# An attention, ELU and expert kernel: attention pairs in undivided blocks, y loads on another queue

## Chip, cores and metric

The kernel runs on one core of a Trainium2 chip. The metric is the device time of one execution in microseconds; a profiled execution gives the trace that is read here.

## What is computed

Three stages follow each other. Attention with a kernel feature map gives 2304 rows of 512; these go through an ELU layer of 2048 hidden units, and the result through four experts of 1024 hidden units, whose outputs are summed with weights.

```python
def phi(x):
    proj = np.einsum('bhsd,df->bhsf', x, w_phi)
    proj = proj - np.max(np.abs(proj), axis=-1, keepdims=True)
    return np.concatenate([np.exp(proj), np.exp(-proj)], axis=-1)
q_p, k_p = phi(q), phi(k)
kv = np.einsum('bhsf,bhsd->bhfd', k_p, v)
z = np.sum(k_p, axis=2)
num = np.einsum('bhsf,bhfd->bhsd', q_p, kv)
den = np.einsum('bhsf,bhf->bhs', q_p, z)[..., None] + 1e-06
attn = num / den                        # 4 batches, 8 heads, 576 rows, 64 columns
...
h = x @ w_in
g = np.where(h > 0.0, h, np.exp(np.minimum(h, 0.0)) - 1.0)
x = g @ w_out
...
p = domain_probs / (domain_probs.sum(-1, keepdims=True) + 1e-09)
for e in range(4):
    out += p[:, e:e + 1] * (np.maximum(x @ w1[e], 0.0) @ w2[e])
```

## The kernel before

Attention works on 16 pairs of heads. For a pair, `mid` projects the last 64 rows of queries and keys together (L229), `keys` and `queries` project the other 512 rows of each into two banks (L237), and for each of these a guard on VectorE subtracts the largest absolute value of a row (L211, L212). ScalarE takes the exponentials of the keys (`kexp`, L215 and L216). `kv` multiplies them with the values (L266, L267), and ScalarE copies the sums to `kvw` (L270). `tpose` transposes the guarded queries (L277, L281), and ScalarE takes their exponentials into `ew` on the way out (L286). `den` multiplies `ew` with the column sums (L295) and `num` with the value part (L308); ScalarE copies both out (`dd` L297, `nd` L309). `den` then sends `dd` to the tile `dn` by a small transfer (L299). `rec` takes the reciprocal on VectorE (L314, L315) and stores it, `spread` loads it back over all partitions into `rb` (L321), and `put_x` multiplies (L327), rounds to `xh` and `xl` (L333, L336) and stores the result. The next pair's queries and keys are loaded inside `queries` into a tile with a single buffer.

The generator `attention` writes these steps out for three pairs at a time: `new` is the youngest, `a` the one ahead of it, `z` the one ahead of that. It yields `True` three times a pair. Pairs 0 to 3 run in a prologue, where TensorE has nothing else, until four results are put; with the fourth, the first ELU tile can run. After that, attention is driven from the ELU units: each unit, 24 matmuls of layer one (L545 to L547) and 24 of layer two (L575 to L577), calls `slot` four times. A slot adds the rate to a quota and runs the generator to its next `True` for each whole one (`RHEAD` for the first two tiles of 256 rows, `RATE` up to tile 5), up to a limit of pairs per tile. A tile has four units; tiles 0 and 1 are interleaved. Slots also drive the conversion of the 64-bit ELU weights, which goes over ScalarE (L121, L122, L155), VectorE (L125 to L130) and GpSimd (L132, L134, L157).

The code is written in that order, and a scheduler then sets each engine's queue from priorities and its own times, so steps can move past each other. TensorE's results go through seven banks, and an ELU tile holds two of them as accumulators.

In the last stage a step is one expert and one group of 768 rows: seven products (L673 to L675) in the place of eight for the first matrix, then `Down` for the second (L777 to L779). For every expert but the first, `Down.run` loads the old sum `y` with a transfer that ScalarE's queue issues (L773), at the moment when the first product of these rows is written; `drain` adds (L787) and stores (L788). The y tiles have four buffers. Expert weights come in over SyncE's queue (`wst`, L480 and L508) and are split on ScalarE and GpSimd (L501, L502, L514, L515).

Of the kernel before, what the change touches and what calls it, by code (L numbers as in the profile page):

```python
# [43 lines left out]
PRE = 0.7  # L44
RATE = 0.375
RHEAD = 0.525
WRATE = 3
# [22 lines left out]
def attn_elu_moe_kernel(ctx: ExitStack, tc: tile.TileContext, kq_in, vv, w_phi, w_in, w_out, probs, w1, w2, out):  # L70
# [150 lines left out]
    class Pair:  # L221
# [4 lines left out]
        def mid(self):  # L226
            self.md = a1.tile([P, 2, P], F32, tag="md", name="md")
            pm = bank()
            pmark[0] = PE.matmul(pm[:, :2 * FEAT], self.kq[:, 512:640], wbd, start=True, stop=True).ins  # L229
            guard(self.md, pm, 2)  # L230
# [110 lines left out]
    def attention():  # L341
        a = new = None
        for i in range(B * NP + 2):
            z, a, new = a, new, Pair(i) if i < B * NP else None
            if a:
                a.kv(0)
                yield False
            if z:
                z.rec()
            if a:  # L350
                a.tpose(0)
                a.kv(1)
                yield False
                a.tpose(1)
                a.tpose(2)
            if new:
                new.mid()
            if a or new:
                yield True
            if z:  # L360
                z.spread()
                yield True
            if new:
                keys = new.keys()
                next(keys)
                yield False
                next(keys, None)
                yield False
            if z:
                z.put_x()  # L370
                done[0] += 1
                yield not new
            if new:
                qs = new.queries()
                next(qs)
                yield False
                next(qs, None)
                yield True
            if a:
                a.den()  # L380
                yield False
                a.num()
                yield False

# [377 lines left out]
    class Down:  # L762
        def __init__(self, e, g, s, j):
            self.e, self.s, self.j = e, s, j
            self.r = (2 * g + s) * NTT + j
            self.acc = None

        def run(self, q):
            if self.acc is None:
                self.acc = bank()  # L770
                self.y = yp.tile([P, DM], F32, tag="y", name="y", bufs=YB)
                if self.e:
                    A.dma_start(self.y, yscr[self.r])  # L773
            c = slice(self.j * P, (self.j + 1) * P)
# [14 lines left out]

    hs = {}  # L790
    xcur = [None]
    steps = [(e, g) for e in range(E) for g in (range(NG) if e % 2 == 0 else range(NG - 1, -1, -1))]
# [140 lines left out]
    for k, (e, g) in enumerate(steps):  # L933
# [8 lines left out]
        for q in range(NQ):  # L942
            if k == q == 0:
                continue
            ups[q].middle()
            slot()
# [89 lines left out]
```

## Time and profile before

| | before |
|---|---|
| median of 3 runs | 1375.21 us (1374.79 to 1375.89) |
| profiled execution | 1369.1 us |
| its span, first to last instruction | 1367.3 us |
| TensorE busy | 1343.6 us |
| VectorE busy | 653.8 us |
| ScalarE busy | 593.9 us |
| GpSimd busy | 353.7 us |

The busy times are of the span; 1.8 us of the profiled execution lie around it. A busy TensorE says that a matmul was in flight, and not that it ran at full speed. Weight loads overlap with matmuls and stand in the profile as an engine of their own, PEld. One matmul of 32-bit data in the attention stage stands as two records.

### The profile page before, as it was taken

How to read it: one execution, taken by the hardware profiler on the slowest of the kernel's cores; microseconds unless marked ns; L12 is line 12 of the kernel's file. 1: busy time of each engine (PE TensorE's matmuls, PEld its weight loads, DVE VectorE, ACT ScalarE, POOL GpSimd, SP SyncE). 2: the span in 40 equal slices, each digit the busy share in tenths (PEclk: the TensorE clock that was granted, in tenths of full speed). 3: DMA queues.
4: the chain of work that ended last, by engine and by line, in shares of the span. 5: the costliest groups of instructions: out<-in, count | busy, mean ns of one | idle time of the engine just before them, and what ended most of it. 6: DMA issues, size and time to landing. Idle time of an engine off the chain costs nothing.

```text
span 1367.3 us, 21606 instructions
## 1 busy us (share of the span) xinstructions
PE 1343.6 (98%) x8408; PEld 1222.4 (89%) x8408; DVE 653.8 (48%) x1085; ACT 593.9 (43%) x1268; POOL 353.7 (26%) x353
## 2 busy tenths in 40 slices
PE   8899999999999999999999999999999999999998
PEld 6788898988999999989888888989898988889897
DVE  5697546564755756683342433233432333433223
ACT  6687555565467554744333351213331213422121
POOL 2487422222454111364110360001420003500000
PEclk9999999999999999999999999999999999999999
DMA  7723344434424313275332155261354241543511
GB/s 245 219 84 94 109 124 155 131 106 125 133 83 123 110 30 121 103 243 177 139 115 106 31 164 194 82 209 44 124 170 162 100 154 31 163 155 99 198 57 62
DMA packets 98422, 173.43 MB, mean 127 GB/s; under 512 B 32272, under 2 KB 45712, under 8 KB 98320
## 3 DMA queue, kind: packets, MB, share of 16 engines
q1 hardware_dynamic: 83392, 148.25, 33.0%
q10 hardware_dynamic: 14928, 23.80, 5.4%
q8 instruction: 66, 1.08, 0.3%
q14 instruction: 36, 0.29, 0.1%
HBM read 118.13 MB, written 53.81 MB: 126 GB/s over the span
## 4 chain that ended last, share of the span: by engine, by line
PE 62%; issue 23%; DVE 3%; DMA 2%; POOL 2%; ACT 1%; SPq 0%; ACTq 0%; POOLq 0%; DVEq 0%
PE bank L673 7%; PE bank L675 7%; PE bank L674 7%; PE bank L777 5%; PE bank L778 5%; PE bank L779 5%; PE bank L266 3%; PE bank L756 2%; PE bank L754 2%; PE bank L755 2%; PE bank L576 2%; PE bank L577 2%; PE bank L545 2%; PE bank L575 2%; POOL w L502 2%
## 5 line engine op out<-in xcount | busy, mean ns | idle before, releaser
L673 PE MATMUL bank<-xv,w 128*128 128x384 f32 x840 | 280.8, 336 | 2.4 <-ACT cm L679 1.2
L674 PE MATMUL bank<-xv,w 128*128 128x384 f32 x840 | 281.6, 335 | 0.0
L675 PE MATMUL bank<-xv,w 128*128 128x384 f32 x840 | 281.5, 336 | 0.0
L778 PE MATMUL bank<-w,h 128*128 128x512 f32 x576 | 227.0, 394 | 0.0
L777 PE MATMUL bank<-w,h 128*128 128x512 f32 x576 | 226.1, 398 | 0.3 <-ACT h L689 0.2
L779 PE MATMUL bank<-w,h 128*128 128x512 f32 x576 | 200.5, 395 | 0.0
L502 POOL TENSOR_TENSOR w<-wst,w 128x256 fp32r<-128x256 f32 x100 | 80.4, 818 | 415.1 <-ACT w L501 415.0
L673 PEld LDWEIGHTS bank<-xv,w 128*128 128x128 f32 x840 | 157.7, 188 | 10.9 <-ACT cm L679 1.9
L674 PEld LDWEIGHTS bank<-xv,w 128*128 128x128 f32 x840 | 157.7, 188 | 6.4 <-POOL xv L624 0.2
L675 PEld LDWEIGHTS bank<-xv,w 128*128 128x128 f32 x840 | 157.6, 188 | 0.1
L689 ACT ACTIVATE h<-bank 128x384 fp32r<-128x384 f32 x144 | 67.8, 489 | 162.4 <-PE bank L675 103.3
L690 DVE SCALAR_TENSOR_TENSOR h<-bank,h 128x384 fp32r<-128x384 f32 x144 | 78.1, 555 | 116.2 <-ACT h L689 115.9
L777 PEld LDWEIGHTS bank<-w,h 128*128 128x128 f32 x576 | 107.8, 188 | 23.3 <-ACT h L689 1.3
L778 PEld LDWEIGHTS bank<-w,h 128*128 128x128 f32 x576 | 108.3, 188 | 22.2
L779 PEld LDWEIGHTS bank<-w,h 128*128 128x128 f32 x576 | 107.6, 188 | 22.2
L687 DVE TENSOR_TENSOR c<-cmab,bank 128x384 f32<-128x384 f32 x48 | 26.6, 554 | 197.5 <-ACT cmab L679 197.5
L679 ACT ACTIVATE cmab<-bank 128x384 f32<-128x384 f32 x60 | 29.4, 490 | 185.4 <-PE bank L675 185.4
L545 PE MATMUL bank<-xh,w 128*128 128x256 f32 x288 | 83.4, 289 | 4.0 <-DVE kp L212 2.2
L624 POOL TENSOR_TENSOR xv<-xs,xv 128x768 fp32r<-128x768 f32 x24 | 46.6, 1943 | 149.7 <-ACT xv L623 143.5
L575 PE MATMUL bank<-gh,w 128*128 128x256 f32 x288 | 82.0, 285 | 0.0
L546 PE MATMUL bank<-xl,w 128*128 128x256 f32 x288 | 81.2, 282 | 0.2 <-POOL xl L336 0.2
L576 PE MATMUL bank<-gl,w 128*128 128x256 f32 x288 | 80.6, 280 | 0.7 <-DVE gl L558 0.7
(118 smaller groups left out, 2531.5 us busy)
## 6 DMA issues: line engine op xcount, KB each, us to landing
xv<-xvd SPq DMA_DIRECT2D x42, 768.0 KB, 4.2
wst<-in_w SPq DMA_DIRECT2D x64, 256.0 KB, 2.8
xvd<-xv SPq DMA_DIRECT2D x21, 768.0 KB, 5.0
yscr<-y SPq DMA_DIRECT2D x54, 256.0 KB, 2.4
y<-yscr ACTq DMA_DIRECT2D x54, 256.0 KB, 2.9
kq<-in_kq SPq DMA_DIRECT2D x16, 320.0 KB, 3.2
rb<-rec SPq DMA_DIRECT2D x32, 144.0 KB, 3.0
xscr<-nd ACTq DMA_DIRECT2D x16, 288.0 KB, 2.8
```

The source lines that it names most:

```text
L502: on[WL[v % len(WL)]].tensor_tensor(out=lo, in0=x, in1=f32(hi), op=ALU.subtract)
L545: PE.matmul(ph[:, j], w[:, 0, c], xh[:, kc], start=(kc == j == 0), stop=False)
L546: PE.matmul(ph[:, j], w[:, 0, c], xl[:, kc], start=False, stop=False)
L575: PE.matmul(o, w[:, 0, c], self.gh[:, j], start=start, stop=False)
L576: PE.matmul(o, w[:, 0, c], self.gl[:, j], start=False, stop=False)
L673: PE.matmul(o, hi[:, c], x[:, 0, kc], start=not more and kc == 0, stop=False, skip_group_check=more)
L674: PE.matmul(o, hi[:, c], x[:, 1, kc], start=False, stop=False, skip_group_check=more)
L675: PE.matmul(o, lo[:, c], x[:, 0, kc], start=False, stop=kc == 1, skip_group_check=more)
L690: mark[0] = V.scalar_tensor_tensor(out=h[:, 1], in0=c, scalar=0.0, in1=f32(h[:, 0]), op0=ALU.max, op1=ALU.subtract).ins
L777: PE.matmul(self.acc, h[:, 0, c], w[:, 0], start=f == 0, stop=False)
L778: PE.matmul(self.acc, h[:, 0, c], w[:, 1], start=False, stop=False)
L779: PE.matmul(self.acc, h[:, 1, c], w[:, 0], start=False, stop=f == 2 * NQ - 1)
```

## The change

One iteration of `attention` is put in another order. It ran value products of `a`, its transposes, `mid` and `keys` of `new`, `queries` of `new`, and then denominators and numerators of `a`, with `rec`, `spread` and `put_x` of `z` and three yields between. Now it runs value products of `a`, `mid` and `keys` of `new`, denominators and numerators of `z`, transposes of `a`, `queries` of `new`, and only then, with the three yields, `rec`, `spread` and `put_x` of `z`. Denominators and numerators are thus computed one iteration later, and all matmuls of an iteration lie between two yields of `True`. `md` gets a second buffer, and both rates are higher. In the last stage `Down.load` takes over the y load: it goes to SyncE's queue, at the start of a step for the first half of the rows and two quarters later for the second, and three tiles of the x pool serve as y buffers beside the four.

```diff
-RATE = 0.375
-RHEAD = 0.525
+RATE = 0.55
+RHEAD = 0.7
...
-            self.md = a1.tile([P, 2, P], F32, tag="md", name="md")
+            self.md = a1.tile([P, 2, P], F32, tag="md", name="md", bufs=2)
...
             if a:
                 a.kv(0)
                 yield False
-            if z:
-                z.rec()
-            if a:
-                a.tpose(0)
                 a.kv(1)
                 yield False
-                a.tpose(1)
-                a.tpose(2)
             if new:
                 new.mid()
-            if a or new:
-                yield True
-            if z:
-                z.spread()
-                yield True
-            if new:
                 keys = new.keys()
                 next(keys)
                 yield False
                 next(keys, None)
                 yield False
             if z:
-                z.put_x()
-                done[0] += 1
-                yield not new
+                z.den()
+                yield False
+                z.num()
+                yield False
+            if a:
+                a.tpose(0)
+                a.tpose(1)
+                a.tpose(2)
             if new:
                 qs = new.queries()
                 next(qs)
                 yield False
                 next(qs, None)
+            yield True
+            if z:
+                z.rec()
                 yield True
-            if a:
-                a.den()
-                yield False
-                a.num()
-                yield False
+                z.spread()
+                yield True
+                z.put_x()
+                done[0] += 1
+                yield not a
...
+        def load(self):
+            if self.e:
+                n = ycount[0] = (ycount[0] + 1) % (YB + XSB)
+                if n < YB:
+                    self.y = yp.tile([P, DM], F32, tag="y", name="y", bufs=YB)
+                else:
+                    self.y = xb.tile([P, 2, TC], F32, tag="xs", name="y", bufs=XSB).rearrange("p a b -> p (a b)")[:, :DM]
+                SP.dma_start(self.y, yscr[self.r])
+            else:
+                self.y = yp.tile([P, DM], F32, tag="y", name="y", bufs=YB)
...
-                self.y = yp.tile([P, DM], F32, tag="y", name="y", bufs=YB)
-                if self.e:
-                    A.dma_start(self.y, yscr[self.r])
+                if self.y is None:
+                    self.load()
...
+            if e and q % 2 == 0:
+                for d in second if q else first:
+                    d.load()
```

TensorE's queue in the prologue, before, from the queries of the third pair on (`kp_478` and `kp_479` are its exponentials of keys, `qd_516` and `qd_517` its guarded queries):

```order
L237 MATMUL bank<-wbd,kq 128x128 x16
L295 MATMUL bank<-ew,kvw 32x288 x8
L308 MATMUL bank<-ew,kvw 64x288 x8
L266 MATMUL bank<-vt_203,kp_478 128x128 x4
L267 MATMUL bank<-vt_203,kpm 128x128
L266 MATMUL bank<-vt_203,kp_478 128x128 x4
L267 MATMUL bank<-vt_203,kpm 128x128
L277 MATMUL bank<-ident,qd_516 128x128
L266 MATMUL bank<-vt_203,kp_479 128x128 x3
L277 MATMUL bank<-ident,qd_517 128x128
```

The same place after (the third pair's exponentials are `kp_418` and `kp_419`, its queries `qd_487` and `qd_488`; the line numbers of these lines are the same):

```order
L266 MATMUL bank<-vt_203,kp_419 128x128 x4
L267 MATMUL bank<-vt_203,kpm 128x128
L229 MATMUL bank<-wbd,kq 128x256
L237 MATMUL bank<-wbd,kq 128x128 x8
L295 MATMUL bank<-ew,kvw 32x288 x8
L308 MATMUL bank<-ew,kvw 64x288 x8
L277 MATMUL bank<-ident,qd_487 128x128
L277 MATMUL bank<-ident,qd_488 128x128
```

The transposes stood among the value products of their own pair; now all value products, the next pair's `mid` and keys (8 of the 16 projections) and an older pair's denominators and numerators stand ahead of them.

VectorE's queue at the same time, before, from the denominators' reciprocal of one pair to the guard of the queries of the fourth pair (`kp_641`, `qd_672`):

```order
L314 TENSOR_SCALAR dn<-dn 128x9
L315 RECIPROCAL dn<-dn 128x9
L211 TENSOR_REDUCE mx<-bank 128x2
L212 TENSOR_TENSOR md<-bank,mx 128x256
L211 TENSOR_REDUCE mx<-bank 128x4 x2
L212 TENSOR_TENSOR kp_641<-bank,mx 128x4x128
L212 TENSOR_TENSOR kp_642<-bank,mx 128x4x128
L125 TENSOR_SCALAR pcs<-pcs 128x512
L327 TENSOR_TENSOR nd<-nd,rb 128x576
L211 TENSOR_REDUCE mx<-bank 128x4 x2
L126 TENSOR_SCALAR pcs<-pcs 128x512
L212 TENSOR_TENSOR qd_672<-bank,mx 128x512
```

And after, from the keys of the fifth pair (`kp_736`, `kp_737`; its queries are `qd_808`, `qd_809`):

```order
L212 TENSOR_TENSOR kp_736<-bank,mx 128x4x128
L129 SCALAR_TENSOR_TENSOR top<-raw,pcs 128x512
L212 TENSOR_TENSOR kp_737<-bank,mx 128x4x128
L130 TENSOR_SCALAR raw<-top 128x512
L327 TENSOR_TENSOR nd<-nd,rb 128x576
L211 TENSOR_REDUCE mx<-bank 128x4 x2
L212 TENSOR_TENSOR qd_808<-bank,mx 128x512
L212 TENSOR_TENSOR qd_809<-bank,mx 128x512
L314 TENSOR_SCALAR dn<-dn 128x9
```

In both, the product of `put_x` (L327) stands between the guards of a block's keys and of its queries. Its own reciprocal (L314) stood ahead of the same block's guards; now it stands behind the query guards of the block before.

ScalarE's queue in a step of the last stage, before, with the y loads in it:

```order
L689 ACTIVATE h<-bank 128x384 x2
L773 DMA y<-yscr_92 128x512
L773 DMA y<-yscr_93 128x512
L773 DMA y<-yscr_94 128x512
L773 DMA y<-yscr_95 128x512
L773 DMA y<-yscr_96 128x512
L679 ACTIVATE cm<-bank 128x384
L689 ACTIVATE h<-bank 128x384
L773 DMA y<-yscr_97 128x512
L679 ACTIVATE cm<-bank 128x384
```

SyncE's queue after, at a change of expert (L771 is the y load, L794 the y store, L476 and L504 the weight loads; 88 to 93 are the rows of the step and of the one behind it):

```order
L476 DMA wst<-in_w 128x512 x4
L794 DMA yscr_88<-y 128x512
L794 DMA yscr_89<-y 128x512
L794 DMA yscr_90<-y 128x512
L771 DMA y<-yscr_88 128x512
L771 DMA y<-yscr_89 128x512
L476 DMA wst<-in_w 128x512
L771 DMA y<-yscr_90 128x512
L504 DMA wst<-in_w 128x512
```

The y loads left ScalarE's queue and stand among SyncE's stores and weight loads.

## Rows read from the trace of the kernel before

**Rows 1.** The page: busy time and instructions of each engine, and TensorE's clock by slices.
```profile
PE 1343.6 (98%) x8408; PEld 1222.4 (89%) x8408; DVE 653.8 (48%) x1085; ACT 593.9 (43%) x1268; POOL 353.7 (26%) x353
...
PEclk9999999999999999999999999999999999999999
```

**Rows 2.** Waits of TensorE: engine, line, releaser; us in total, times, longest.
```profile
PE bank L277 <- DVE qd L212: 3.9, 3, 2.4
PE bank L545 <- DVE kp L212: 2.2, 1, 2.2
PE bank L545 <- ACT xh L333: 1.8, 1, 1.8
...
PE bank L673 <- ACT cm L679: 1.2, 2, 0.8
```

**Rows 3.** Timeline of TensorE: start, us, instruction, and in brackets idle time before it.
```profile
16.02 0.60 PE L229 MATMUL bank<-wbd,kq 128*128 128x256 f32 x2
...
27.39 0.60 PE L229 MATMUL bank<-wbd,kq 128*128 128x256 f32 x2
...
30.23 1.18 PE L295 MATMUL bank<-ew,kvw 128*32 128x288 f32 x16
...
33.43 1.16 PE L266 MATMUL bank<-vt,kp 128*128 128x128 f32 x8
...
39.73 0.60 PE L229 MATMUL bank<-wbd,kq 128*128 128x256 f32 x2
...
52.13 0.30 PE L277 MATMUL bank<-ident,qd 128*128 128x128 f32 x1 [2.40 <-DVE qd L212]
...
55.89 0.94 PE L229 MATMUL bank<-wbd,kq 128*128 128x256 f32 x2
...
68.96 0.60 PE L229 MATMUL bank<-wbd,kq 128*128 128x256 f32 x2
...
88.46 0.28 PE L546 MATMUL bank<-xl,w 128*128 128x256 f32 x1
...
88.93 0.28 PE L547 MATMUL bank<-xh,w 128*128 128x256 f32 x1
...
96.92 0.36 PE L545 MATMUL bank<-xh,w 128*128 128x256 f32 x1 [2.19 <-DVE kp L212]
```

**Rows 4.** Timeline of VectorE between 46 and 53 us.
```profile
48.83 0.76 DVE L327 TENSOR_TENSOR nd<-nd,rb 128x576 f32<-128x576 f32 x1 [2.00 <-DMA rb<-rec]
49.50 1.28 DVE L211 TENSOR_REDUCE mx<-bank 128x4 f32<-128x512 f32 x2
...
51.30 1.28 DVE L212 TENSOR_TENSOR qd<-bank,mx 128x512 f32<-128x512 f32 x2
```

**Rows 5.** Windows: stretch, its length, busy us of each engine, PEclk, DMA share, GB/s.
```profile
50.00:60.00 10.00, 7.87 (x74) 6.56 (x74) 6.69 (x15) 6.68 (x18) 6.53 (x7) 0.83 0.67 198
92.00:102.00 10.00, 7.81 (x75) 7.15 (x77) 9.70 (x15) 8.24 (x17) 9.88 (x9) 0.83 0.26 89
10.00:70.00 60.00, 54.88 (x524) 45.13 (x526) 41.23 (x79) 42.81 (x97) 21.37 (x23) 0.97 0.71 222
70.00:130.00 60.00, 57.67 (x530) 51.05 (x529) 49.95 (x84) 48.84 (x104) 49.50 (x46) 0.97 0.31 93
```

**Rows 6.** Timelines of ScalarE and VectorE: `dd` of two pairs, `put_x` of the later.
```profile
33.85 0.39 ACT L297 ACTIVATE dd<-bank 128x288 f32<-128x288 f32 x1
...
61.08 0.39 ACT L297 ACTIVATE dd<-bank 128x288 f32<-128x288 f32 x1
...
73.92 0.76 DVE L327 TENSOR_TENSOR nd<-nd,rb 128x576 f32<-128x576 f32 x1 [0.15 <-DMA rb<-rec]
```

**Rows 7.** Lines of ScalarE: count, busy us, mean ns of one, idle before.
```profile
L286 ACT ACTIVATE ew<-bank 128x512 f32<-128x512 f32 (+1 forms) x96 | 40.4, 499 | 22.2 <-PE bank L277 22.2
...
L215 ACT ACTIVATE kp<-kp 128x512 f32<-128x512 f32 x32 | 19.8, 629 | 29.1 <-DVE kp L212 29.0
```

**Rows 8.** Waits of ScalarE: the longest for a y load.
```profile
ACT cm L679 <- DMA y<-yscr: 13.1, 1, 13.1
```

More of the change, by code (lines that the diff above doesn't have):

```diff
@@ L765, in __init__ @@
             self.r = (2 * g + s) * NTT + j
-            self.acc = None
+            self.acc = self.y = None
+        def load(self):
[8 more added lines that the diff above has]
+                self.y = yp.tile([P, DM], F32, tag="y", name="y", bufs=YB)
         def run(self, q):
@@ L790, in attn_elu_moe_kernel @@
     hs = {}
+    ycount = [0]
     xcur = [None]
```

## Prediction

> **What bounds the kernel now.** I read the page first, then who TensorE (PE) waited for, then the start-up on PE's timeline, then windows around the two longest waits, then the engines that feed PE there. On the page PE is busy for 1343.6 of 1367.3 us, and no slice is below 0.8 [rows 1]. The change leaves the set of matmuls as it is (each line issues as many as before), so it can only take away or add waits and lower clock. All PE idle time is 1367.3 - 1343.6 = 23.7 us, and that bounds the gain. The waits named [rows 2] are few: transposes for the query guard on VectorE (DVE) 3.9, a first ELU matmul for the key guard 2.2, another for x on ScalarE (ACT) 1.8, the last stage twice for a copy on ACT, 1.2.
>
> Most of it is at the start. In the prologue only attention runs; each pair's block begins with the `mid` projection (L229), at 16.02, 27.39, 39.73, 55.89 and 68.96 us [rows 3]. The intervals are 11.37, 12.34, 16.16 and 13.07; with the first as the clean length, the other three lose 0.97 + 4.79 + 1.70 = 7.46. Inside the long one stands the chain to follow: `put_x` on DVE waited 2.00 for the spread reciprocals, the query guards stand behind it in DVE's queue and begin at 49.50 [rows 4], and the transposes of these queries start at 52.13 after 2.40 of idle PE [rows 3]. Then the clock fell: over 50 to 60 us it is 0.83 in the mean, so 1.7 us of full speed (2.4 against 1.2 GHz) are lost, and over 92 to 102, around the 2.2 wait, another 1.7 [rows 5]. After the 1.8 and 1.2 waits the row of PEclk shows no fall [rows 1].
>
> **Part by part.**
>
> *Denominators and numerators one pair later.* Before, pair p's denominators come at the end of its own block, and its `put_x` must be over before the query guards of p+2. From the copy `dd` at 33.85 to `put_x` at 48.83 is 15.0 us [rows 4, 6], two small transfers and two broadcasts. PE's work from that pair's denominators (30.23) to the end of the next query projections was: products of denominators and numerators 3.2 (30.23 to 33.43), value products and transposes 5.5 to 5.7, projections 2.5 to 2.8 [rows 3], 11.4 in all; from the earliest possible `dd`, 1.6 later, 9.8. So the chain is some 5 too long, and PE pays part of that at the transposes. Now `put_x` of a pair follows the key guards of the block after the one with its denominators: `mid` and keys stand ahead of the denominators, and between them and the next query projections' end lie 3.2 + 1.1 + 1.2 + 4.5 + 0.5 + 1.2 + 3.2 + 1.1 + 1.2 = 17.2, from `dd` 15.6. That covers 15.0. A late guard costs less, too: from query projections to their own transposes PE had about 6 us and now has 4.5 + 1.7 + 3.2 = 9.4, against 2.6 of guards (two pieces of 1.28 each [rows 4]).
>
> *Value products after more work.* From a pair's key projections to its value products PE had the query projections and 3.2; now 3.2, transposes 1.1, queries 1.2. That helps except in the first block, where there is no older pair: only 1.1 + 1.2 = 2.3 remain. ACT does the six exponentials of the transposes first (about 2.5 for a pair, 96 in 40.4 [rows 7]), after two of `mid` (0.8); then the first key exponential, 0.63 [rows 7]. From the end of the key projections that is 0.8 + 2.5 + 0.63 = 3.9 against 2.2 to 2.3: a new wait of 1.7, once. Ends: 0.5 if ACT starts early, and 2.4 with 1.7 of clock behind it if this wait is like the one at 52.13. I take 1.7, nearest to the ACT rows.
>
> *Rest of the prologue.* The next pair's keys load only after this pair's query projections and are wanted after 4.5 us of value products instead of 8 to 9. That is near the load itself; I take 0.5 (0 to 1.5). Three blocks keep 0.3 each of small pauses: 0.9. The prologue then loses 1.7 + 0.5 + 0.9 = 3.1 instead of 7.46: gain 4.4. ACT and DVE had 42.8 and 41.2 us of work in 60 [rows 5], so in 55 they still fit.
>
> *First ELU tile.* Its last quarter needs pair 3's `put_x`. That took 12.8 from `dd` before (61.08 to 73.92 [rows 6]), out of sight behind a whole block. Now pair 3's denominators stand directly ahead, and PE has queries 1.2, transposes 1.1, 18 ELU matmuls 2.1, value products 4.5, `mid` and keys 1.7, and 3 to 4 of the next denominators and numerators, with 2 of its own numerators 14 to 15 in all. ACT has key exponentials ahead of `dd`, some 2 to 3 us. New wait: 1.0, ends 0 and 2.9, with 1.7 of clock on top at the far end.
>
> *The wait at 96.92.* Before, keys and queries of a pair were projected in one stretch, four banks at once, and the ELU matmul at 96.92 waited for a bank that the key guard still read [rows 2, 3]; DVE, with weight conversions ahead of the guard, was busy for 9.70 of 10 us there [rows 5]. Now 5.5 us of other work stand between key projections and query projections. Wait and clock were 2.2 + 1.7 = 3.9; I leave 1.0 of it: gain 2.9 (0 to 3.9).
>
> *Higher rates (0.55, 0.7).* Pairs need three slots either way, so they come sooner by slots, until the limit per tile. The last pair's denominators stand 168 ELU matmuls ahead of tile 6 instead of 48, and another 30 or 18 precede the first use of its x. At 0.118 us (four starts from 88.46 to 88.93 [rows 3]) the cover grows from 78 matmuls, 9.2, to 186, 22; the chain took 12.8 to 15.0 [rows 4, 6]. The 1.8 wait [rows 2] goes: gain 1.8. Next late is the guard work on DVE of the tiles behind it, which does not move.
>
> *y loads.* Fifty-four move from ACT's queue to SP's and go out a step early, with seven buffers. ACT once stood 13.1 us at such a load [rows 8], but no PE wait in that stage is over 0.8 [rows 2], and those two come at changes of expert, behind weight pieces whose order on ACT stays. On SP, stores and weight loads (`wst`) stand behind a load that waits for the store of its own rows: at two changes of expert that may delay a weight. I take 0, ends +1.2 (both of these waits [rows 2]) and -3.
>
> *Undivided pieces.* About ten blocks of 11 us now stand among ELU matmuls without one inside. I take 0.1 each, 1.0 in all (0 to 8, see the first rival).
>
> Sum: 4.4 - 1.0 + 2.9 + 1.8 + 0 - 1.0 = 7.1. The profiled execution took 1369.1 (span and 1.8 around it), 6.1 under the median of the runs, 1375.2; I carry the difference over: 1362.0 for such an execution, **1368.1** for the median.
>
> **Rivals.**
>
> *Banks run out in the undivided block* (slower). A block fills twelve banks in 11 us; seven exist, and the ELU accumulators hold two. If DVE or ACT is behind with conversions, PE waits inside each block with nothing else to issue. For it: the 96.92 wait was of that kind, and DVE was busy for 49.95 of 60 us from 70 to 130 [rows 5]. Against it: by the order now built, key banks have 5.5 us to be emptied. Without the 1.0 that I took for it the gain is 8.1, so it decides from 0.81 a block. At 1.2 a block it costs 12: 1375.2 - 8.1 + 12 = 1379.
> The Trainium skill, "TensorE: Matmul & The Clock Gate", section "A second HAM failure mode: psum-queue depth-cycling", says that short PE idles between groups of matmuls, from cycling through PSUM banks, can make the clock swing between its two levels. By that rule each of ten blocks would add one fall like those seen, 17 us: near 1392. The trace does not bear it out so far: falls follow only the two waits over 2.1 us.
>
> *The side engines set the prologue's pace* (no change). The reciprocal waits in DVE's queue for its transfer, ahead of the next guards; if that holds each block at 12.9, four blocks lose 6 of the 7.46, the first ELU wait takes 2.9 and the rest brings 4: gain 1 to 2, 1373.5.
>
> *Nearly every wait goes.* 7.46 + 3.9 + 1.8 = 13.2 with little back: 1362 to 1364.
>
> **How the numbers follow.** About 0.2%, 2.75 us, is what a measurement of this kernel tells from no change. Forecast (1364.5 to 1372): 0.56. Nearly all waits gone: 0.09. Pace unchanged: 0.20. Slower by banks, or by SP's queue: 0.15. Faster 0.65, same 0.20, slower 0.15. The range, 1363.5 to 1377, takes in the no-change case and leaves out most of the slower one and the best end.
>
> **What would show it.** In the changed profile `mid` should start every 11.4 to 11.9 us from its third time on, without a wait of transposes for the query guard; a wait of about 1.7 should stand before the second pair's value products near 18.5; ELU should begin near 66 instead of 70.6; no wait for x near 335; and the waits of the last stage should stay. I am wrong if waits for DVE or ACT recur once a block between 70 and 330 us, if the clock falls more than twice, or if weights arrive late at 805, 985 or 1175.

## The result and the profile after

The change made the kernel slower: 1384.29 us in the median of six runs (1383.0 to 1388.15) against 1375.43 (1374.13 to 1377.37) in runs of before beside them, a ratio of 1.0068 with a 95% interval of 1.0056 to 1.0081. The forecast was 1368.1 with a range to 1377. The profiled execution took 1383.0, its span 1381.2.

The page of after, busy time and instructions, which answers to [rows 1]:

```profile
PE 1357.2 (98%) x8408; PEld 1230.2 (89%) x8408; DVE 657.9 (48%) x1085; ACT 592.6 (43%) x1268; POOL 354.1 (26%) x353
```

The span grew by 13.9 us, and TensorE's busy time by 13.6. Idle time is 24.0 us, as it was (23.7). With the same 8408 records the engine was busy for longer, so the loss isn't in the sum of the waits. Most of the added busy time stands at one line, though the experiments will show that this line's busy time overstates what it costs. Busy time of L237 alone (the projections) in the kernel before, by windows; columns are window, its length, busy time (records), granted clock, DMA share, GB/s:

```profile
0.00:72.00 72.00, 13.36 (x176) 0.98 0.72 224
72.00:340.00 268.00, 22.25 (x336) 0.99 0.38 117
```

The same in the kernel after:

```profile
0.00:72.00 72.00, 17.38 (x192) 1.00 0.70 219
72.00:340.00 268.00, 31.33 (x322) 0.99 0.38 113
```

In sum the 512 records of the projections kept TensorE busy for 48.72 us in place of 35.61, 13.1 more. TensorE's timeline shows how (start, length, instruction, count; idle time in brackets). Before, a pair's keys and queries among ELU products:

```profile
229.97 2.06 PE L237 MATMUL bank<-wbd,kq 64*128 64x128 f32 x32
231.95 0.39 PE L545 MATMUL bank<-xh,w 128*128 128x256 f32 x1
```

After, queries alone, at two places:

```profile
127.95 1.16 PE L237 MATMUL bank<-wbd,kq 64*128 64x128 f32 x8
129.40 1.16 PE L237 MATMUL bank<-wbd,kq 64*128 64x128 f32 x8 [0.30 <-ACT nd L309]
130.49 0.39 PE L571 MATMUL bank<-gh,w 128*128 128x256 f32 x1
...
179.67 1.71 PE L237 MATMUL bank<-wbd,kq 64*128 64x128 f32 x16
181.31 0.39 PE L541 MATMUL bank<-xh,w 128*128 128x256 f32 x1
```

From start to the start of the next work, 32 records took 1.99 us before; after, 16 take 1.64 at 179.67 and 2.54 at 127.95. (The keys of such pairs take 1.09.) Two heads share a projection, one on rows 0 to 63 of the array, the other on rows 64 to 127. Record by record, two neighbours on different halves start 6 or 7 ns apart and the next two 105 later; on the same half each record starts 112 after the last. The queue as built holds the heads of a group in this order (0 and 1 are the halves):

```
before, most groups          01010101 01010101
after, most keys             01010101
after, most queries          00001111
```

Neighbours on the same half stand 6 times in the queue of before and 72 times in that of after. The two banks of a projection are no longer free at the same time, since three transposes and three products of denominators and numerators now stand directly ahead, each with a bank. So the scheduler issues first what needs the first bank alone. How far the second bank really came late, the second run below shows.

The longest waits after, which answer to [rows 2]:

```profile
PE bank L572 <- DVE gl L554: 2.9, 2, 2.3
PE bank L571 <- ACT gh L553: 1.9, 1, 1.9
PE bank L266 <- ACT nd L309: 1.9, 1, 1.9
...
PE bank L266 <- ACT kp L215: 1.2, 1, 1.2
PE bank L277 <- ACT dd L297: 1.2, 1, 1.2
```

The waits for `qd`, `kp` (L545), `xh` and `cm` are gone, and others have come. Two of them end in low clock; two windows of after (busy time of PE, PEld, DVE, ACT, POOL, then granted clock), to be held against [rows 5]:

```profile
100.00:115.00 15.00, 12.91 (x82) 11.05 (x81) 13.08 (x24) 12.26 (x28) 12.91 (x13) 0.77 0.29 81
354.00:372.00 18.00, 13.16 (x87) 12.56 (x86) 15.62 (x19) 7.45 (x13) 9.41 (x6) 0.81 0.41 124
```

Each loses 3.4 us of full speed (0.23 x 15, 0.19 x 18). The waits in the second window stand in the last ELU units. VectorE there, after:

```profile
358.94 1.79 DVE L114 TENSOR_TENSOR pr<-pr,prr 128x72 f32<-128x72 f32 x1
360.65 0.67 DVE L129 SCALAR_TENSOR_TENSOR top<-w,pcs 128x512 uint32<-128x512 uint32 x1
361.25 0.68 DVE L552 SCALAR_TENSOR_TENSOR g<-g,bank 128x512 f32<-128x512 f32 x1
...
363.05 0.42 DVE L130 TENSOR_SCALAR w<-top 128x512 uint32<-128x512 uint32 x1
363.39 0.41 DVE L484 TENSOR_TENSOR wst<-wst 128x256 f32<-128x256 f32 x1
363.72 1.52 DVE L554 TENSOR_TENSOR gl<-g,gh 128x512 fp32r<-128x512 f32 x1
```

A weight conversion (L125 to L130) stands among expert weights (L484), x splits and the ELU's own `g` and `gl` (L552, L554), for which TensorE waits. Before, the last conversion was over at 343.5.

### The profile page after: what moved, and what is told of

Same layout as the page of the kernel before. It is cut to its first block, busy times and chain, and to the rows that moved or that the text cites. A ratio compares the mean times of both kernels' runs of the same rounds, so it can differ in the third digit from the quotient of the medians.

```text
span 1381.2 us, 21496 instructions
## 1 busy us (share of the span) xinstructions
PE 1357.2 (98%) x8408; PEld 1230.2 (89%) x8408; DVE 657.9 (48%) x1085; ACT 592.6 (43%) x1268; POOL 354.1 (26%) x353
## 3 DMA queue, kind: packets, MB, share of 16 engines
q10 hardware_dynamic: 7152, 9.64, 1.9%
## 4 chain that ended last, share of the span: by engine, by line
PE 84%; DMA 5%; DVE 5%; ACT 3%; issue 2%; SPq 0%; ACTq 0%; POOL 0%; DVEq 0%; POOLq 0%
PE bank L669 10%; PE bank L671 10%; PE bank L670 10%; PE bank L783 10%; PE bank L785 10%; PE bank L784 9%; PE bank L266 3%; PE bank L752 2%; PE bank L750 2%; PE bank L751 2%; PE bank L237 2%; PE bank L571 2%; PE bank L572 2%; PE bank L573 2%; PE bank L541 2%; PE bank L542 2%
## 5 line engine op out<-in xcount | busy, mean ns | idle before, releaser
L571 PE MATMUL bank<-gh,w 128*128 128x256 f32 x288 | 82.9, 288 | 1.9 <-ACT gh L553 1.9
L573 PE MATMUL bank<-gh,w 128*128 128x256 f32 x288 | 81.9, 284 | 0.0
```

Source lines behind the costliest of these rows:

```text
L571: PE.matmul(o, w[:, 0, c], self.gh[:, j], start=start, stop=False)
L573: PE.matmul(o, w[:, 1, c], self.gh[:, j], start=False, stop=stop)
```

## The experiments

Ratios are to before on the same chip; there before took 1372.1 to 1372.2 us in the median. A ratio is an estimate with an interval of its own and not the quotient of the two medians, from which it differs by up to 0.0014. Behind the first row each run has 11 or 12 executions, but "halves alternating" has six and the last two have four. "L237 busy" is the busy time of the projections between 0 and 340 us, as above. The last column is from the one profiled execution, and it includes the start: in "conversions sooner", "two dn" and "put behind queries" the first value products took 2.04 or 2.05 us in place of 1.13 in before and after, and the second pair's `mid` started late, at 16.67, 16.45 and 17.74 (16.02 in before, 14.87 in after).

| run | ratio (95%) | us | L237 busy | first ELU product at |
|---|---|---|---|---|
| before / after | 1 / 1.0068 (1.0056, 1.0081) | 1375.4 / 1384.3 | 35.61 / 48.72 | 70.58 / 71.94 |
| halves apart, in before | 1.0037 (1.0023, 1.0052) | 1377.4 | 49.20 | 73.98 |
| halves alternating, in after | 1.0077 (1.0049, 1.0105) | 1382.5 | 43.21 | 71.77 |
| old rates, in after | 1.0013 (0.9999, 1.0028) | 1374.1 | 46.63 | 72.63 |
| new rates, in before | 1.0025 (1.0009, 1.0040) | 1375.8 | 35.85 | 72.55 |
| y loads, in before | 0.9970 (0.9954, 0.9987) | 1368.6 | 35.48 | 71.48 |
| order alone | 1.0040 (1.0022, 1.0058) | 1379.4 | 44.84 | 75.57 |
| queries behind keys | 1.0028 (1.0014, 1.0042) | 1376.8 | 37.45 | 79.26 |
| denominators first | 1.0046 (1.0032, 1.0060) | 1378.4 | 37.71 | 79.51 |
| conversions sooner, in after | 1.0029 (1.0016, 1.0043) | 1376.9 | 47.88 | 76.28 |
| two dn, old rates | 0.9996 (0.9980, 1.0012) | 1373.0 | 46.60 | 73.67 |
| put behind queries, y loads | 0.9891 (0.9868, 0.9915) | 1359.1 | 36.16 | 69.23 |
| the same with two dn | 0.9893 (0.9870, 0.9915) | 1359.3 | 35.07 | 69.06 |

### What the order of the halves costs

In the kernel before, each projection issues all of one head first:

```diff
-            for t in range(4):
-                for h in range(2):
+            prev = None
+            for h in range(2):
+                for t in range(4):
                     r = slice(h * D, h * D + D)
-                    pmark[0] = PE.matmul(...).ins
+                    with tc.issue_after(prev) if prev is not None else nullcontext():
+                        prev = PE.matmul(...).ins
+            pmark[0] = prev
```

> The kernel before, with one edit: in a projection all products of one head are issued ahead of all products of the other, in a fixed order. The products of head 0 use rows 0 to 63 of the array and those of head 1 rows 64 to 127. Theory A (products of opposite halves run at the same time when they alternate, and lose that when they stand apart): a stretch of 32 records took 1.99 us in the trace of before; in the trace of after 16 records took 1.09 alternated and 1.64 to 2.0 apart, so 32 would take 3.1 to 3.6, and 15 pairs at full clock cost 1.1 to 1.6 each. Part of it falls into waits that the prologue has anyway. Expected: 12 to 24 us slower than before, 1387 to 1399. Rival B (the order of the halves is free, and the 13.5 us that these lines gained from before to after are waits and low clock): 1375 to 1377, and stretches of 32 stay at 1.99.

The same stretch of 32 records as above, now in the run with the halves apart:

```profile
235.81 2.82 PE L239 MATMUL bank<-wbd,kq 64*128 64x128 f32 x32
238.56 0.39 PE L548 MATMUL bank<-xh,w 128*128 128x256 f32 x1
```

It takes 2.75 us from start to start instead of 1.99, in every unsplit stretch at full clock. The mechanism of theory A is shown; its size was too high (0.76 a pair, since the last three records of one group and the first of the next still overlap, against 1.1 to 1.6), and of the 13.6 us that L237 is busier only 5.1 come out in the time (1372.1 x 0.0037). So the order of the halves has a price, and L237's busy time overstates it.

Then, in the kernel after, the products are chained in alternating order (the same chain, with the old two loops):

> The kernel after, with one edit: the products of a projection are chained, so that the two heads alternate in every group. Theory A1 (the scheduler's order of the halves is the loss, and the second bank is free soon enough): groups of 16 that took 1.49 to 2.5 us take 1.09, 6 to 8 us in all come back, near 1377. Theory A2 (the second bank is free only about half a microsecond after the first; the order of the halves is how the lack of banks is paid): the groups take 1.09, but a wait of 0.2 to 0.5 for a copy or an exponential of ScalarE stands ahead of most of them; 0 to 3 us come back, 1381 to 1384. Rival B (order is free): 1384, groups unchanged in length.

TensorE's timeline at the place shown above for after (127.95):

```profile
127.64 0.49 PE L239 MATMUL bank<-wbd,kq 64*128 64x128 f32 x2
129.09 1.16 PE L239 MATMUL bank<-wbd,kq 64*128 64x128 f32 x14 [0.97 <-ACT nd L312]
130.18 0.39 PE L574 MATMUL bank<-gh,w 128*128 128x256 f32 x1
```

The group still takes 2.54 us: it now waits 0.97 for the copy `nd` to free the second bank. L237 is busy for 5.5 us less than in after, with 2.3 us of waits on it in place of 0.5, and the ratio's interval holds after's. So the 6 to 8 us of A1 are excluded. A2 holds in part. Such a wait stands at three of the 16 groups of queries (0.97, 0.52 and 0.84), and there the lack of a bank is the cause, and the order of the halves is how it was paid. It does not stand "ahead of most of them": at five others, from 178 us on, the group alternates without a wait, in 1.09 to 1.25 us where after took 1.64. That so little of this comes out in the time stays open; the interval is 3.8 us wide to either side.

### Rates, y loads and the order, one by one

Three runs lead from before to after: the order alone, then with the y loads (that is after with the old rates), then with the rates (after).

```diff
-RATE = 0.55
-RHEAD = 0.7
+RATE = 0.375
+RHEAD = 0.525
```

> The kernel after, with the two rates of before (0.375 and 0.525). In the order as built VectorE's queue then has all weight conversions ahead of the expert weights' and the x splits of the last ELU units, as before; with the higher rates two conversions stand among them. Theory C (the rates cause the waits of layer two and the fall of the clock at 354 to 371 us): these waits (4.9 us over the usual) and the fall (6.8 us at half clock, 3.4 lost) go, the wait for x near 338 (1.8) may come back: 1376 to 1379. Rival D (the cluster comes from the new order of an iteration, through the number of steps that the prologue drives the weight conversion): it stays, 1383 to 1385.

> The kernel before, with the two rates of after (0.55 and 0.7) and nothing else. Theory C: the wait for x near 338 goes (1.8), and a cluster of waits for g, gh or gl with a fall of the clock appears in the last ELU units, 6 to 8: 1379 to 1382. Rival D: only the wait for x goes: 1373 to 1374.5. The projections should keep their order and cost the same as before in either case.

With the old rates the kernel after takes 1.0013: 7.5 us of its loss go with two constants. TensorE in the last ELU units, with the old rates (columns as for the two windows above):

```profile
352.00:374.00 22.00, 22.00 (x189) 22.00 (x189) 16.56 (x20) 12.44 (x19) 8.52 (x5) 1.00 0.51 154
```

The same window in after:

```profile
352.00:374.00 22.00, 17.16 (x121) 16.56 (x120) 19.07 (x24) 8.23 (x13) 11.04 (x7) 0.84 0.37 113
```

The new rates alone cost the kernel before 3.4 us (3.6 to 6.6 expected). Waits for `gl` stand in the last ELU units, 1.56 ahead of 351.6 and 1.30 ahead of 358.9, but without a fall of the clock there. The longest new wait, for `g`, ends at 102.7, and a fall begins beside it (0.77 granted between 95 and 110):

```profile
PE bank L308 <- DVE g L556: 3.3, 1, 3.3
PE bank L576 <- DVE gl L558: 2.9, 2, 1.6
```

Rival D falls. Theory C holds in the kernel after; in before its waits came, but its fall of the clock came elsewhere, at the wait for `g`. What the rates do in after, the next run asks: with the new rates kept, conversions are driven faster, so that in VectorE's queue they end ahead of the x splits.

```diff
-WSLOW = 1.3
+WSLOW = 1.6
```

> The kernel after with its new rates; only the rate of the weight conversion between tile 2 and tile 5 is raised (1.3 to 1.6), so that the last conversion stands ahead of the x splits in VectorE's queue as built, while the x splits stay as early as in after. Theory C1 (the two conversions that stand among x splits and expert weights delay g and gl, and so make the waits and the fall of the clock at 354 to 371 us): most of the 7 us comes back, ratio to before 1.000 to 1.003. Rival C2 (the x splits, earlier by a unit because the last pairs come earlier, do it themselves): waits and fall stay, ratio 1.005 to 1.008.

Its window is full again, and 5.4 us come back (1.0068 to 1.0029):

```profile
352.00:374.00 22.00, 22.00 (x190) 22.00 (x189) 15.16 (x18) 9.87 (x17) 7.16 (x4) 1.00 0.31 96
```

So C1 holds: with higher rates the last pairs, and with them the x splits, came a unit sooner, the conversions didn't, and the two met in VectorE's queue ahead of `g` and `gl`. What doesn't come back is the other fall: this run still has one of 3.4 us near 110, as after has near 105, and the run with the old rates has none.

> The kernel before, with only the y loads of after (SyncE's queue, a step early, seven buffers). In the trace of after the waits of L673 for cm at 987 (0.77 us) and 1177 (0.47) are gone, and the last stage is 1.6 shorter from start to start. Theory: this is the y part's own gain, 1.2 to 1.6 us faster than before, a ratio near 0.999. Rival (it comes from the shifted schedule ahead, or SyncE's queue delays weights in exchange): the two waits stay, or others of 0.5 to 1.2 appear near 805, 985 or 1175; ratio 1.000 to 1.001.

> The new order of an iteration and the second md buffer alone: the rates and the y loads of before. After with old rates took a ratio of 1.0013 to before, and y is worth -0.001. Theory E (the new order by itself costs: projections lose their concurrency and are split, +10.7 us by their lines, against about 9 that waits and low clock give back): a ratio of 1.0015 to 1.0035, 2 to 5 us slower than before, projections at 48 to 49 us in sum against 37.8. Rival F (the order is neutral, and all of the loss is the rates'): 0.9995 to 1.0010.

The y loads alone bring 4.1 us (1.8 to 6.3), more than expected. The two waits for `cm`, 1.2 us in before, are gone, as in after; what makes up the rest isn't shown. The run with the order alone keeps ScalarE's y loads, and has three, 2.8 us in all:

```profile
PE bank L669 <- ACT cm L675: 2.8, 3, 1.1
```

The order alone costs 5.5 us (3.0 to 8.0): theory E, a little over its range. "Order alone" here and below takes in the second buffer of `md`, which no run has by itself. Why it doesn't cost the 9 to 11 us that L237 is busier was worked out from the records, by adding up for each line the time from every record's start to the next one's. The run with the y loads alone and after with the old rates differ in the order (and `md`) alone, and neither has a fall of the clock. Between them projections take 9.64 us more, `mid` 2.82, the transposes of `md` 1.84, other transposes 1.61 and denominators 1.51. Value products take 6.38 less and ELU products 5.29 less. With 0.10 of the rest that is 5.85 more, against spans of 1370.2 and 1364.4.

`mid` and the transposes of `md` became slower by their neighbours alone. Sixteen `mid`s in place of six now stand directly ahead of a projection, and this starts 0.309 us after the start of the last record of `mid`; an ELU product starts 0.028 after it. Of the value products' gain, 5.5 are the waits for query guards. The ELU products stood 25 times directly ahead of projections or denominators, with 0.206 to the next start, and now once; among themselves they start 0.121 apart before and 0.119 now, and for that no row gives a reason.

### Queries back behind the keys

From after with the old rates; queries stand behind the keys of their pair, then denominators, numerators, transposes. In the second run denominators and numerators stand ahead of `mid` instead.

```diff
                 next(keys, None)
                 yield False
+            if new:
+                qs = new.queries()
+                next(qs)
+                yield False
+                next(qs, None)
+                yield False
             if z:
                 z.den()
...
                 a.tpose(2)
-            if new:
-                qs = new.queries()
-                next(qs)
-                yield False
-                next(qs, None)
```

> After with the old rates, and in an iteration queries stand directly behind keys again, ahead of the denominators, numerators and transposes. In the order as built, products of the same half stand next to each other 24 times in place of 66, and 13 of 16 pairs have their 32 records in one stretch. Theory G (stretches and halves make the 10.7 us): 0.19 for each of some 13 stretches joined, 0.09 for each of 42 neighbours, so projections fall from 48.5 us to 40 to 43 and the time by 4 to 7 against after with the old rates: ratio to before 0.996 to 0.9985. Rival H (four banks at a time are not free then either, and TensorE waits for guards or copies instead): projections 46 or more with waits inside, ratio 1.000 to 1.003.

> As the run with queries behind keys, but denominators and numerators of the pair in front stand ahead of mid and keys, and transposes last. 38 neighbours of the same half. Theory G: projections at 41 to 44 us, ratio 0.997 to 0.9995. Rival H: 46 or more, ratio 1.000 to 1.003. The four projection banks come directly behind the three of denominators and numerators here, so if ScalarE's copies set when banks come free, this one is slower than the run with queries behind keys by 1 to 3 us.

L237 falls to 37.45 (37.71 in the second run), even below what theory G said, but the time doesn't fall: 1.0028, and 1.0046 for the second. So theory G is right on this line and wrong on the time: the busy time of the projections isn't what the order costs in the end. The waits moved, above all in the prologue; the run with queries behind keys:

```profile
PE bank L266 <- ACT nd L309: 3.8, 1, 3.8
PE bank L542 <- ACT nd L309: 2.4, 1, 2.4
PE bank L277 <- DVE kp L212: 1.7, 2, 1.2
```

ELU begins at 79 us instead of 72.6. Of H the time came true in the first run, not the place; the second run is slower than either theory said, and 2.5 us slower than the first, as expected if copies set when banks come free, though the two intervals overlap. In the first run the waits are at transposes, value products and ELU products behind. It looks as if a small number of banks is paid in one way or another, but no run has another number of banks, so that is argued and not shown.

### One buffer of dn

A wait of value products for `nd` stands near 59 to 62 in five of these traces: 1.88 us in after, 1.47, 1.10, 3.46 and 3.44 with halves alternating, old rates, the order alone and conversions sooner. ScalarE's queue in after:

```profile
56.35 0.55 ACTq L299 DMA_DIRECT2D dn<-dd  x1
56.94 0.63 ACT L216 ACTIVATE kp<-kp 128x512 f32<-128x512 f32 x1 [1.62 <-DMA rec<-dn]
...
58.58 0.69 ACT L309 ACTIVATE nd<-bank 128x288 f32<-128x288 f32 x2
```

And TensorE:

```profile
59.03 1.16 PE L266 MATMUL bank<-vt,kp 128*128 128x128 f32 x8 [1.88 <-ACT nd L309]
```

The transfer from `dd` waits at the head of ScalarE's queue until the pair ahead has stored its reciprocals out of the same `dn`, and the copies behind it wait too. With two buffers:

```diff
-            self.dn = a1.tile([P, S // D], F32, tag="dn", name="dn")
+            self.dn = a1.tile([P, S // D], F32, tag="dn", name="dn", bufs=2)
```

> After with the old rates, and the tile dn in two buffers. In the trace of after ScalarE issues the transfer from dd to dn at 42.80, 56.35 and 69.89 us, 13.5 apart as the blocks of the prologue are, and its queue stood 1.62 us for the store of the pair ahead out of the same dn, with the copies nd behind it and TensorE's wait of 1.88 at 59.03 behind those. Theory K (this one buffer sets the pace of the prologue in the new order): no wait for nd near 59, no fall of the clock in the first 70 us, the first ELU product 1 to 3 us earlier than in after with old rates (72.6), and 1 to 3 us less in time: ratio 0.999 to 1.0005 against 1.0013. Rival L (the store of the pair ahead is late because the reciprocal is, and the next wait takes its place): the first ELU product at 72 to 73, ratio 1.001 to 1.002.

ScalarE with two buffers; nothing stands between the transfer and the copy but an exponential of keys, which waited for their guard:

```profile
55.92 0.55 ACTq L299 DMA_DIRECT2D dn<-dd  x1
56.66 0.63 ACT L215 ACTIVATE kp<-kp 128x512 f32<-128x512 f32 x1 [0.77 <-DVE kp L212]
57.20 0.39 ACT L309 ACTIVATE nd<-bank 128x288 f32<-128x288 f32 x1
```

The wait near 59 is gone, so that buffer made it. But waits for `kp` (0.3, ending at 62.9) and `kvw` (1.1, ending at 70.1) took its place, and ELU began at 73.67, not sooner. The last doesn't speak against theory K: the second pair's `mid` started at 16.45 in place of 14.79 with one buffer, ahead of any `dn`, so from there on this run is 0.6 us shorter. The ratio, 0.9996, is better than 1.0013, but the intervals overlap: what the buffer is worth in time stays open.

### The chain of put_x, in the old order

The forecast read in [rows 4] that query guards stand behind a `put_x` that waits. This run does only what that reading asks for: the order of before, with the y loads, and `put_x` behind the queries.

```diff
-            if z:
-                z.put_x()
-                done[0] += 1
-                yield not new
             if new:
                 qs = new.queries()
                 next(qs)
                 yield False
                 next(qs, None)
                 yield True
+            if z:
+                z.put_x()
+                done[0] += 1
+                yield not new
```

> The kernel before with the y loads of after, and put_x of the pair in front stands behind the query guards instead of ahead of them; all else in the old order. It takes up the reading that the multiplication waiting for rb holds the query guards, and TensorE's transposes behind them. If that is the chain, the waits of the transposes for qd (5.5 us in the run with the y loads alone) fall to 1 or less, the first ELU product comes at 67 to 69 in place of 71.5, and the time falls by 2 to 4 us: ratio to before 0.9945 to 0.9960 against 0.997. Rival: the denominators' copy, or the key guards, end last instead; the first ELU product stays at 71 to 73 and the ratio at 0.9965 to 0.999.

> As the run with put_x behind the queries, and the tile dn in two buffers. If in that order the transfer from dd to dn waits for the store of the pair ahead (it came a block later), the second buffer is worth 1 to 2 us over the run without it: ratio 0.993 to 0.9955. If not, both runs are alike within 1 us.

VectorE in the prologue of that run, which answers to [rows 4]:

```profile
48.18 0.68 DVE L212 TENSOR_TENSOR qd<-bank,mx 128x512 f32<-128x512 f32 x1
48.78 0.69 DVE L125 TENSOR_SCALAR pcs<-pcs 128x512 f32<-128x512 f32 x1
49.38 0.68 DVE L212 TENSOR_TENSOR qd<-bank,mx 128x512 f32<-128x512 f32 x1
50.24 1.88 DVE L327 TENSOR_TENSOR nd<-nd,rb 128x576 f32<-128x576 f32 x1 [0.18 <-DMA rb<-rec]
```

The guards are over before the multiplication, which waits 0.18 in place of 2.00. TensorE's waits for `qd` are down to one:

```profile
PE bank L277 <- DVE qd L212: 0.3, 1, 0.3
```

It takes 1359.1 us, 13.0 less than before and 9.6 less than with the y loads alone, by the medians (15.0 and 10.8 by the ratios), and beats both kernels. Far more came than expected. ELU began 2.3 sooner (71.48 to 69.23), and from there to the last ELU product it took 5.4 less (343.6 to 338.2): the wait for `kp`, 2.5 in the run with the y loads, went too, and 15 of 16 pairs have their projections in one group. Idle TensorE time is 15.9 us in place of 24.6. The two profiled executions differ by 6.7 us only (spans 1357.7 and 1364.4). Much of the rest is in the clock: the profiled execution with the y loads alone has no fall, but over its twelve executions the granted clock is 0.9974 in the mean, and over the four of this run 0.9998. Of 1368 us that difference makes about 3, as an estimate, near the 2.9 that are missing. A second `dn` adds nothing here, as the second of the two branches expected.

## Why the prediction was wrong

| term | forecast | measured |
|---|---|---|
| new order (4.4 - 1.0 + 2.9 - 1.0) | 5.3 faster | 5.5 slower (order alone) |
| y loads | 0 | 3.7 faster (order alone to after with old rates) |
| higher rates | 1.8 faster | 7.5 slower (from there to after) |
| sum | 7.1 faster | 9.3 slower |

*The premise failed first.* "The change leaves the set of matmuls as it is, so it can only take away or add waits and lower clock." The same projections kept TensorE busy for 13.1 us more by their order and neighbours, which neither a wait nor an idle row shows; in time the order as a whole cost 5.5 where 5.3 were to be gained. The order as built showed it: 72 neighbours on one half in place of 6, and projections split in groups (two of 1.09 for one of 1.99, 0.19 for each pair). The bound by idle time held for the gains, and was useless for the loss. That is also why none of the signs named in the prediction came: between 70 and 330 us no wait recurred once a block, the clock fell twice and not more, and no weight was late. The forecast was wrong by something that the list didn't hold.
The Trainium skill, "TensorEngine Tiling (Array Packing)", section "Tiling Modes", says that a change of tiling mode drains TensorE; by that each more switch between full-height and half-height products costs. The trace agrees as far as there is a cost at such places (0.19 a split; 0.309 from `mid` to a projection against 0.028 to an ELU product). The same page of the Trainium skill, section "Restrictions and Gotchas", adds that row tiles press on PSUM, since each half writes to a bank of its own; the three groups that wait for `nd` when the order is forced are that case. The Trainium skill, "TensorE: Matmul & The Clock Gate", section "Part 3: Packing small matmuls — row/col tiling", says that matmuls start and end strictly in queue order. The trace doesn't agree for the starts: in the group at 179.67, built as 0000 1111, the second half's first record starts at 180.22 and the last record of the first half, ahead of it in the queue, at 180.55. The two halves overlap by three records, and no more: the group takes 1.64 and not 1.09.

*The rival of banks had part of the cause, and the wrong payment.* I looked for a wait in each undivided block, found 5.5 us between key and query projections enough to empty the keys' banks, and took 0.1 a block. But the queries' banks come from transposes and numerators directly ahead, not from the keys. Waits inside most blocks did stay away, as did a fall of the clock in each: it fell twice in all, so what the prediction gave 1392 for has no support here.

*Higher rates.* The wait for x near 335 went, as forecast; but it is gone with the old rates too, so in the new order there was nothing left for the rates to gain. "The guard work on DVE of the tiles behind it, which does not move" was wrong: x splits moved ahead of two conversions, and waits of 0.64, 1.93 and 2.28 with a fall of the clock cost more than that wait. A fall cost 3.4 us here, twice the 1.7 that I had from [rows 5]. Most of the 7.5 is clock: over all executions 0.9943 is granted in after and 0.9978 with the old rates, which is close to 5 us, as an estimate. (The row of PEclk in [rows 1], from which the prediction reads that no fall followed the shorter waits, shows a 9 at the two falls too. The reading is right, but by windows: 1.00 around each of those waits.)

*Prologue.* The chain was read rightly, as the run with `put_x` moved shows: transposes no longer wait for `qd`. The wait before the second pair's value products came at 1.2 (forecast 1.7). But from its third time on `mid` started at 23.60, 37.05, 49.38 and 62.48, so 12.3 to 13.5 apart and not 11.4 to 11.9, and ELU began at 71.94, not 66. The term that was too small is TensorE's own work. In after one block has no idle time at all:

```profile
37.05 0.60 PE L229 MATMUL bank<-wbd,kq 128*128 128x256 f32 x2
...
43.10 1.71 PE L237 MATMUL bank<-wbd,kq 64*128 64x128 f32 x16
44.74 1.16 PE L266 MATMUL bank<-vt,kp 128*128 128x128 f32 x8
...
49.38 0.60 PE L229 MATMUL bank<-wbd,kq 128*128 128x256 f32 x2
```

It takes 12.33 us. The prediction's own terms for a block, with keys and queries at 1.2 each and transposes at 1.1, make 11.7; queries took 1.64 (0000 1111) and transposes 1.23. Its waits ahead of the first ELU product add up to 4.1 us, 5.9 in before, so that even without them ELU would begin near 68. The rival with blocks of 12.9 had the pace, but not the reason. One wait was not costed at all: `dn`, whose one buffer is now asked for again before it is stored (1.88 at 59.03).

*The wait at 96.92* went, and two for `md` and `dd` (0.85 and 1.24) with the first fall of the clock took its place at 102 to 105: a gain of 2.9 that was given back a block later. With the old rates there are waits at that place too (0.85, 0.51 and 0.66), but no fall.

*y loads.* The zero was a term of the wrong size. The waits for `cm` did depend on the y loads ahead of them in ScalarE's queue, though ScalarE's order of weight pieces is unchanged. The ends that I gave were 1.2 faster and 3 slower, so the 3.7 lies outside them.

## What to carry to other kernels

Before treating a set of matmuls as unchanged, look at which halves of the array neighbours use and how often full-height and half-height products alternate; TensorE's busy time can grow with no wait in sight. If a chain is read in the profile, move the one step that breaks it and keep the rest: moving one step with its yield gave 9.6 us here, where a whole new order around the same step lost 5.5. A rate that brings one stream of work sooner makes it meet another, so look at what stands in each queue where the stream ends.

## What the runs showed of the hardware

Products on rows 0 to 63 and 64 to 127 started 6 or 7 ns apart where they alternate, and 112 ns apart on the same half at full clock. Where one half is issued ahead of the other, the second half's first record still started ahead of the last three of the first half. A projection directly behind `mid` started 0.309 us after the start of the last record of `mid`, an ELU product 0.028. Falls of the clock cost 1.7 us each in before and 3.4 in after. And a small VectorE operation was long while GpSimd worked: in after `pr` times `prr`, 128x72, ran from 358.94 to 360.73 (1.79 us; 0.23 in before), beside this one of GpSimd, which ended at 360.63:

```profile
358.79 1.84 POOL L620 TENSOR_TENSOR xv<-xs,xv 128x768 fp32r<-128x768 f32 x1
```
